# Gate products, the output weight's split and the maxima visits take other places in the prologue of a gated Fourier and attention kernel

## The chip, the cores and the metric

The kernel runs on one core of one Trainium2 chip. Its time is the device time of one execution in microseconds; the time before is the median of three runs.

## The reference

The reference mixes one sequence of 2048 rows of 512 numbers, all in float32, in two ways and blends the results by a gate.

```python
g = _sigmoid((x * gate_w).sum(-1, keepdims=True))
a = dft_seq_re @ (x @ dft_hid_re.T) - dft_seq_im @ (x @ dft_hid_im.T)
q, k, v = heads(x @ wqkv)                  # 32 heads of 16
b = merge(softmax(q @ k.T * 16**-0.5) @ v) @ wo
out = g * a + (1 - g) * b
```

(The lines are shortened; `heads` and `merge` stand for the transposes.)

## The kernel before, in words

Every product in the Fourier part and the projections is made from two parts of each operand, a rounded high part and the rest (`hi_lo`, lines 74 to 76: ScalarE casts the high part, VectorE or GpSimd subtracts for the low part), with three matmuls for each pair (`mm3`, lines 78 to 81). A chain is the twelve matmuls of one 128 x 512 result tile over the four pieces of the inner dimension.

The order of work on every engine is that in which the program issues it; there is no scheduler. The prologue goes in these stages.

1. **q and k**: for each of four blocks of 512 rows (`tb`), four chains of q and four of k. Weights and transposed x come through six `raw` buffers (`staged`, lines 93 to 96) and are split between the chains (`split`, lines 106 to 113; the list of them ends with the imaginary half's weights `wch` and `wcl`). `evac_qk` (lines 136 to 140) splits each result into one of seven `hl` buffers and stores it in DRAM. The gate weights, one row broadcast to 128 partitions (`gwb`), are loaded behind the last chain (line 175).
2. Between the stages SP issues two rows of x for the gate, one of wo, and `load_stacks(0)` (lines 183 to 192): twelve loads that put q and k of the first pair of heads into `qs` and `ks`.
3. **v**: sixteen chains with `wv` (lines 259 to 268); each result is copied to `vt`, one half by ScalarE and one by VectorE.
4. **The imaginary half**: sixteen chains with `wch` (lines 280 to 301). Each result `b` is split into one of two `hl` buffers of a second pool and stored. Behind the b row stands the gate product of row block s on VectorE (line 293, x times `gwb`, summed into column s of `z`) and the load of block s + 2. Behind chains 2 to 5 a piece of wo is split by ScalarE and GpSimd into one of the same two `hl` buffers and stored, and the next is loaded. From the seventh chain on `split(1)` splits a piece of the real half's weights `wre`, which take the memory of `wv`.

`visit(i)` (lines 247 to 257) is called behind chain i of v (0 to 15) and of the imaginary half (16 to 31). From i = 10 on it issues four products of q and k (line 204, 128 x 512 each, three into the banks of `psA` and one into that of `psD`) whose row maxima VectorE takes (line 206); 22 such visits, 44 pairs of tiles, make the lead that the main loop wants. Finished maxima are turned and put beside q by two deferred steps (`m_parts`, `m_rows`), which visits run.

Then the main loop begins with the real half's chains (line 343, into the one bank of `psD`), scores, maxima and values interleaved, and the sequence transform after that. The gate itself is computed once at its beginning (`gate`, lines 611 to 617).

Matmul results go through eight banks: three `s` (`psS`), three `a` (`psA`), one for the values and one `d`. The SP queue issues nearly all transfers, in program order; a transfer that must wait for an engine holds up those behind it.

Of the kernel before, what the change touches and what calls it, by code (L numbers as in the profile page):

```python
# [9 lines left out]
F32 = mybir.dt.float32  # L10
F32R = mybir.dt.float32r
AF = mybir.ActivationFunctionType
ALU = mybir.AluOpType
AX = mybir.AxisListType

P = 128
S = 2048
D = 512
# [3 lines left out]
KT = D // P  # L22
NT = S // P
UNITS = NP * 32
LEAD = 44
# [6 lines left out]
def mix_kernel(ctx: ExitStack, tc: tile.TileContext, xa_t, xa, wqkv, w_hid, w_seq, wo, gate_w, out):  # L32
# [5 lines left out]
    nc = tc.nc  # L38
# [17 lines left out]
    wo_d = [dram.tile([P, 2, D], F32, name=f"wo{kt}") for kt in range(KT)]  # L56
# [5 lines left out]
    z = const.tile([P, NT], F32, name="z")  # L62
# [11 lines left out]
    def hi_lo(hi, lo, src, lo_eng=None):  # L74
        nc.scalar.copy(hi, src)  # L75
        (lo_eng or nc.vector).tensor_tensor(lo, src, hi.bitcast(F32), ALU.subtract)  # L76

    def mm3(ps, sh, sl, mh, ml, first, last):
        nc.tensor.matmul(ps, sh, mh, start=first, stop=False)  # L79
        nc.tensor.matmul(ps, sh, ml, start=False, stop=False)  # L80
        nc.tensor.matmul(ps, sl, mh, start=False, stop=last)  # L81

    right = tc.tile_pool(name="st1", bufs=1, side="right", reuse_waits="tile")
    st1 = right.__enter__()
# [4 lines left out]
    gwb = st1.tile([P, D], F32, name="gwb")  # L89

    todo, loaded = [], []

    def staged(src):
        raw = st1.tile([P, D], F32, name="raw", bufs=RAW)
        nc.sync.dma_start(raw, src)
        return raw

    def add(hi, lo, src, lo_eng, shape=None):
        todo.append((hi, lo, src, lo_eng, shape))

    def load_ahead():
        while todo and len(loaded) < RAW - 1:
            hi, lo, src, lo_eng, shape = todo.pop(0)
            loaded.append((hi, lo, staged(src), lo_eng, shape))

    def split(n):

        for _ in range(n):
            load_ahead()
            if loaded:  # L110
                hi, lo, raw, lo_eng, shape = loaded.pop(0)
                hi_lo(hi, lo, raw.rearrange("p (s t) -> p s t", s=4) if shape else raw, lo_eng)
            load_ahead()

    def add_x(tb, kt):
        x = xab[tb][:, :, :, kt * P:(kt + 1) * P]
        add(x[:, :, 0], x[:, :, 1], xa_t[tb, :, kt], nc.vector, True)
# [3 lines left out]
    def bank():  # L121
        nonlocal banks
        banks += 1
        return (psS if banks % 2 else psA).tile([P, 512], F32, name="s" if banks % 2 else "a")


    with tc.tile_pool(name="qk", bufs=1, reuse_waits="tile") as pool:
        wh = pool.tile([P, 2, KT, D], F32R, name="wh")
        wl = pool.tile([P, 2, KT, D], F32R, name="wl")

        def mm_qk(ps, c, ct, tb, kt):
            cols = slice(ct * P, (ct + 1) * P)
            x = xab[tb][:, :, :, kt * P:(kt + 1) * P]
            mm3(ps, wh[:, c, kt, cols], wl[:, c, kt, cols], x[:, :, 0], x[:, :, 1], kt == 0, kt == KT - 1)

        def evac_qk(ps, c, ct, tb):
            hl = pool.tile([P, 2, D], F32R, name="hl", bufs=7)
            hi_lo(hl[:, 0], hl[:, 1], ps)
            nc.sync.dma_start(qk_d[c][:, ct * P:(ct + 1) * P, tb * 512:(tb + 1) * 512].rearrange("v p t -> p v t"),
                              hl.bitcast(F32))  # L140

        for kt in range(KT):
            add(wh[:, 0, kt], wl[:, 0, kt], wqkv[0, :, kt], nc.vector)
            add_x(0, kt)
        for kt in range(KT):
            add(wh[:, 1, kt], wl[:, 1, kt], wqkv[1, :, kt], nc.vector)
        for tb in range(1, 4):
            for kt in range(KT):
                add_x(tb, kt)
        for kt in range(KT):  # L150
            add(wv[0][kt], wv[1][kt], wqkv[2, :, kt], nc.gpsimd)
        for kt in range(KT):
            add(wch[:, kt], wcl[:, kt], w_hid[1, :, kt], nc.gpsimd)
        split(8)
        nc.vector.memset(acc, 0.0)

        for tb in range(4):
            for c in range(2):
                if tb == 0 and c == 0:
                    pss = [bank() for _ in range(4)]  # L160
                    for kt in range(KT):
                        for ct in range(4):
                            mm_qk(pss[ct], c, ct, tb, kt)
                    split(4)
                    for ct in range(4):
                        evac_qk(pss[ct], c, ct, tb)
                    continue
                for ct in range(4):
                    ps = bank()
                    for kt in range(KT):  # L170
                        mm_qk(ps, c, ct, tb, kt)
                    split(1 if ct % 2 and tb else 2)
                    evac_qk(ps, c, ct, tb)
        split(len(todo) + len(loaded))
        nc.sync.dma_start(gwb, gate_w.broadcast_to([P, D]))

    main = ctx.enter_context(tc.tile_pool(name="main", bufs=1, reuse_waits="tile"))

# [4 lines left out]
    def load_stacks(p):  # L183
        q_t, k_t = qs[p % 2], ks[p % 2]
        for h in range(2):
            rows = slice((2 * p + h) * DH, (2 * p + h + 1) * DH)
            o = 64 * h

            for i, (qv, kv) in enumerate(((0, 0), (0, 1), (1, 0))):
                part = slice(o + 16 * i, o + 16 * i + 16)  # L190
                nc.sync.dma_start(q_t[part].bitcast(F32), qk_d[0][qv, rows])
                nc.sync.dma_start(k_t[part].bitcast(F32), qk_d[1][kv, rows])
# [37 lines left out]
    def run_deferred():  # L230
        while deferred:
            deferred.pop(0)()
# [5 lines left out]
    for i in range(2):  # L238
        for h in range(2):
            for tb in range(2):  # L240
                nc.gpsimd.dma_start(ks[i][64 * h + 48:64 * h + 50, tb * 2 * D:(tb + 1) * 2 * D].bitcast(F32), ones)
    xgs = {s: staged(xa[s]) for s in range(2)}
    wos = [staged(wo[:, 0])]
    load_stacks(0)
    a_next = 0

    def visit(i):

        nonlocal a_next
        if i < 10 or a_next == LEAD:  # L250
            return
        if deferred:
            deferred.pop(0)()
        for j in range(2):
            for h in range(2):
                a_tile(a_next, h, psD.tile([P, 512], F32, name="d") if j and h else None)
            a_next += 1

    for s in range(NT):
        t = xab[s // 4][:, s % 4]  # L260
        ps = psS.tile([P, 512], F32, name="s")
        for kt in range(KT):
            r = slice(kt * P, (kt + 1) * P)
            mm3(ps, t[:, 0, r], t[:, 1, r], wv[0][kt], wv[1][kt], kt == 0, kt == KT - 1)
        visit(s)
        pv = ps.rearrange("p (r h d) -> p r h d", h=2, d=DH)
        nc.scalar.copy(vt[:, s, :, 0:16], pv[:, :, 0])
        nc.vector.tensor_copy(vt[:, s, :, 17:33], pv[:, :, 1])

    def spare(i, dt, name):  # L270

        return const.tile([P, 4, P], dt, name=name, tag=f"w{i}")


    wre = [[const.tile([P, D], F32R, name=f"wre{v}{kt}", tag=f"w{4 * v + kt}") for kt in range(KT)] for v in range(2)]
    for kt in range(KT):
        add(wre[0][kt], wre[1][kt], w_hid[0, :, kt], nc.gpsimd)

    ab = [xab[s // 4][:, s % 4] for s in range(NT)]
    for s in range(NT):  # L280
        t = ab[s]
        ps = psS.tile([P, 512], F32, name="s")
        for kt in range(KT):
            r = slice(kt * P, (kt + 1) * P)
            mm3(ps, t[:, 0, r], t[:, 1, r], wch[:, kt], wcl[:, kt], kt == 0, kt == KT - 1)
        visit(NT + s)
        bt = st1.tile([P, 2, D], F32R, name="hl", bufs=2)
        hi_lo(bt[:, 0], bt[:, 1], ps)
        nc.sync.dma_start(b_d[s], bt.bitcast(F32))
        if s + 2 < NT:  # L290
            xgs[s + 2] = staged(xa[s + 2])
        xg = xgs.pop(s)
        nc.vector.scalar_tensor_tensor(xg, xg, 1.0, gwb, op0=ALU.mult, op1=ALU.mult, accum_out=z[:, s:s + 1])
        if 2 <= s < 2 + KT:
            wt = st1.tile([P, 2, D], F32R, name="hl", bufs=2)
            hi_lo(wt[:, 0], wt[:, 1], wos.pop(0), nc.gpsimd)
            nc.sync.dma_start(wo_d[s - 2], wt.bitcast(F32))
            if s + 1 < 2 + KT:
                wos.append(staged(wo[:, s - 1]))
        elif s >= 2 + KT:  # L300
            split(1)
    run_deferred()
    assert a_next == LEAD
    right.__exit__(None, None, None)
# [108 lines left out]
    oh, yp, wos = {}, {}, []  # L413
# [441 lines left out]
```

## Time and profile before

| | us |
|---|---|
| median of 3 runs | 1752.51 |
| the runs | 1752.32 to 1754.02 |
| the profiled execution | 1753.26 |
| its span, first to last instruction | 1751.5 |

The profile is one execution. Its page gives the busy time of each engine; PE is TensorE's matmuls, PEld its weight loads, DVE VectorE, ACT ScalarE, POOL GpSimd, SP the engine that issues transfers. Its tables of stretches give, for each stretch, every engine's busy time with the count of instructions, the TensorE clock that was granted (PEclk, 1.00 is full), the mean busy share of the 16 DMA engines and the GB/s they moved. A row of the waits reads: engine, line, tile, what it waited for, us in total, times, longest. A row of the timeline reads: start, duration, engine, line, operation, result and operands, shape, count, and in brackets the idle time before it with what ended it. Matmuls are pipelined: the distance between starts, not the duration, is what one costs.

### The profile page before, as it was taken

To read this page: it belongs to the slowest core of one execution; us is meant where nothing else is said; L and a number is where in the kernel's file an instruction comes from. 1 tells how busy PE (TensorE), PEld (TensorE's weight loads), DVE (VectorE), ACT (ScalarE), POOL (GpSimd) and SP (SyncE) were. 2 spreads that over 40 slices of the span, in tenths; PEclk is the share of its full clock that TensorE was granted. 3 is DMA by queue.
4 is the path that set the end of the run, shared out by engine and by line. 5 is a ranking of instruction groups with operands and counts; after the bars stand their busy time and mean duration, and the time that the engine had idled before them with its cause. 6 is when DMAs were issued, how large, how long until landed. Compare 5 with 4: busy or idle time off the path is not lost.

```text
span 1751.5 us, 32890 instructions
## 1 busy us (share of the span) xinstructions
PE 1727.6 (99%) x12721; PEld 1042.1 (59%) x12721; DVE 1368.1 (78%) x2302; ACT 1153.6 (66%) x2257; POOL 447.0 (26%) x561
## 2 busy tenths in 40 slices
PE   8999999999999999999999999999999999999998
PEld 7886554456666666656666666666666566544443
DVE  5228878888888888888888888888888888899953
ACT  5211267776776777776767777767767777777776
POOL 0110222232223233222223243333323333200111
PEclk9999899999999999999999999999999999999999
DMA  8754630304133152414146443314141535461113
GB/s 291 234 113 138 224 42 7 56 21 78 44 62 67 45 123 80 86 55 79 38 80 211 107 127 98 72 57 86 44 85 56 129 98 98 146 168 26 38 27 127
DMA packets 82348, 164.79 MB, mean 94 GB/s; under 512 B 19712, under 2 KB 19968, under 8 KB 78352
## 3 DMA queue, kind: packets, MB, share of 16 engines
q1 hardware_dynamic: 77840, 162.30, 36.4%
q8 instruction: 100, 1.64, 0.4%
q0 software_dynamic: 4352, 0.39, 0.3%
q14 instruction: 56, 0.46, 0.1%
HBM read 107.47 MB, written 54.52 MB: 92 GB/s over the span
## 4 chain that ended last, share of the span: by engine, by line
PE 93%; DVE 2%; ACT 2%; DMA 1%; issue 0%; DVEq 0%; SPq 0%; ACTq 0%
PE d L343 35%; PE acc L638 26%; PE s L629 11%; PE a L204 11%; PE s L79 2%; PE s L80 2%; PE s L81 2%; DVE mx L206 1%; ACT pt L630 1%; DMA b<-hl 1%; PE a L79 1%; PE a L80 1%; PE a L81 1%; ACT y L359 0%; DVE hl L76 0%
## 5 line engine op out<-in xcount | busy, mean ns | idle before, releaser
L206 DVE TENSOR_REDUCE mx<-a 128x1 f32<-128x512 f32 x2026 | 1244.4, 681 | 243.3 <-PE a L204 229.5
L630 ACT ACTIVATE pt<-s 128x512 f32<-128x512 f32 x2008 | 1025.5, 622 | 391.2 <-PE s L629 333.7
L204 PE MATMUL a<-ks,qs 48*128 48x512 f32 x2026 | 814.4, 418 | 3.1 <-DVE mx L206 2.4
L629 PE MATMUL s<-qs,ks 50*128 50x512 f32 x2008 | 769.7, 413 | 0.9 <-ACT pt L630 0.8
L343 PE MATMUL d<-xab,ch 64*128 64x512 f32 x2016 | 648.7, 396 | 0.0
L638 PE MATMUL acc<-pt,vt 128*17 128x512 f32 x4096 | 500.3, 596 | 0.0
L343 PEld LDWEIGHTS d<-xab,ch 64*128 64x128 f32 x2016 | 365.9, 184 | 126.3 <-DVE mx L206 60.4
L629 PEld LDWEIGHTS s<-qs,ks 50*128 50x128 f32 x2008 | 365.6, 184 | 109.1 <-ACT pt L630 30.8
L204 PEld LDWEIGHTS a<-ks,qs 48*128 48x128 f32 x2026 | 366.8, 185 | 77.2 <-DVE mx L206 48.4
L343 PE MATMUL d<-xab,cl 64*128 64x512 f32 x1008 | 399.5, 396 | 0.0
L343 PEld LDWEIGHTS d<-xab,cl 64*128 64x128 f32 x1008 | 185.5, 184 | 64.9 <-DVE mx L206 40.8
L327 POOL CAST ch<-craw 128x512 fp32r<-128x512 f32 x126 | 77.1, 612 | 555.2 <-PE a L204 177.6
L638 PEld LDWEIGHTS acc<-pt,vt 128*17 128x17 f32 x4096 | 90.1, 96 | 206.0 <-issue 206.0
L328 POOL TENSOR_TENSOR cl<-craw,ch 128x512 fp32r<-128x512 f32 x126 | 162.1, 1287 | 10.2
L227 POOL DMA_DIRECT2D qs<-mt x128 | 72.0, 568 | 160.1 <-DVE mt L223 151.6
L343 PE MATMUL d<-wre,xab 64*128 64x512 f32 (+1 forms) x348 | 95.1, 406 | 5.0 <-ACT pt L630 2.5
L343 PEld LDWEIGHTS d<-wre,xab 64*128 64x128 f32 (+1 forms) x348 | 59.9, 185 | 42.6 <-issue 26.1
L343 PE MATMUL d<-wo_hl,o_hl 64*128 64x512 f32 (+1 forms) x261 | 71.0, 398 | 0.0
L343 PEld LDWEIGHTS d<-wo_hl,o_hl 64*128 64x128 f32 (+1 forms) x261 | 47.1, 185 | 15.9 <-issue 11.7
L75 ACT CAST hl<-s 128x512 fp32r<-128x512 f32 x32 | 18.7, 585 | 56.8 <-PE s L81 49.5
L76 DVE TENSOR_TENSOR hl<-s,hl 128x512 fp32r<-128x512 f32 x32 | 22.0, 687 | 35.0 <-ACT hl L75 35.0
L218 POOL CAST nhl<-nm 128x16 fp32r<-128x16 f32 x32 | 6.3, 197 | 151.2 <-DVE nm L215 151.2
(125 smaller groups left out, 931.8 us busy)
## 6 DMA issues: line engine op xcount, KB each, us to landing
craw<-w_seq SPq DMA_DIRECT2D x128, 256.0 KB
qk<-hl SPq DMA_DIRECT2D x32, 512.0 KB
qs<-qk SPq DMA_DIRECT2D x96, 128.0 KB
ks<-qk SPq DMA_DIRECT2D x96, 128.0 KB
b<-hl SPq DMA_DIRECT2D x16, 512.0 KB
xab<-b SPq DMA_DIRECT2D x16, 512.0 KB
o<-oe SPq DMA_DIRECT2D x62, 128.0 KB
oh<-nh SPq DMA_DIRECT2D x12, 512.0 KB
```

What stands on the lines that cost most here:

```text
L79: nc.tensor.matmul(ps, sh, mh, start=first, stop=False)
L80: nc.tensor.matmul(ps, sh, ml, start=False, stop=False)
L81: nc.tensor.matmul(ps, sl, mh, start=False, stop=last)
L204: nc.tensor.matmul(ps, qs[p % 2][r, qt * P:(qt + 1) * P], ks[p % 2][r, kb * 512:(kb + 1) * 512], start=True, stop=True)
L206: user = nc.vector.tensor_reduce(mx[p % 2][:, h, qt, kb:kb + 1], ps, AX.X, ALU.max)
L227: (nc.sync, nc.gpsimd)[h].dma_start(rows.rearrange("v (q b c) -> v b q c", q=8, b=4)[:, b], mt[hf][32 * b + h:32 * b + 32:2])
L327: nc.gpsimd.tensor_copy(h1, raw)
L328: nc.gpsimd.tensor_tensor(l1, raw, h1.bitcast(F32), ALU.subtract)
L343: i = nc.tensor.matmul(self.ps, st[r], mv[r], start=not self.begun, stop=stop)
L629: nc.tensor.matmul(ps, ks[p % 2][rr, kt * P:(kt + 1) * P], qs[p % 2][rr, q0:q0 + 512], start=True, stop=True)
L630: return nc.scalar.activation(pts[u][:, 2 * qb + h], ps, AF.Exp, bias=0.0, scale=DH ** -0.5)
L638: nc.tensor.matmul(acc[32 * j:32 * j + 17], vt[:, kt, p, 16 * h:16 * h + 17], pt[:, j], start=kt == 0, stop=kt == NT - 1)
```

## The change

- The gate products move from behind the chains of the imaginary half to behind the last sixteen chains of q and k. The gate weights and five rows of x are loaded ahead of those chains, and each product is followed by the load of the row block five further on.
- The splits of wo move from behind chains 2 to 5 of the imaginary half to behind chains 6, 8, 10 and 12 of v; their four loads are issued together behind `load_stacks(0)`. Behind each store of a wo piece a piece of the real half's weights is loaded, and these are split behind the first four chains of the imaginary half.
- The visits issue maxima from i = 7 on instead of i = 10; their number stays 22, so the last is behind chain 28 and not 31. A visit runs a deferred step even when it has no maxima to issue.

```diff
+        xgs = {}
+        def gate_row(s):
+            xg = xgs.pop(s)
+            nc.vector.scalar_tensor_tensor(xg, xg, 1.0, gwb, op0=ALU.mult, op1=ALU.mult, accum_out=z[:, s:s + 1])
+            if s + 5 < NT:
+                xgs[s + 5] = staged(xa[s + 5])
+
         for tb in range(4):
+            if tb == 2:
+                assert not todo and not loaded
+                nc.sync.dma_start(gwb, gate_w.broadcast_to([P, D]))
+                xgs.update({s: staged(xa[s]) for s in range(5)})
...
                     evac_qk(ps, c, ct, tb)
-        split(len(todo) + len(loaded))
-        nc.sync.dma_start(gwb, gate_w.broadcast_to([P, D]))
+                    if tb > 1:
+                        gate_row(8 * (tb - 2) + 4 * c + ct)
...
-    xgs = {s: staged(xa[s]) for s in range(2)}
-    wos = [staged(wo[:, 0])]
     load_stacks(0)
+    wos = [staged(wo[:, kt]) for kt in range(KT)]
+    wrs = []
...
     def visit(i):
-        if i < 10 or a_next == LEAD:
-            return
         if deferred:
             deferred.pop(0)()
+        if i < 7 or a_next == LEAD:
+            return
...
         nc.vector.tensor_copy(vt[:, s, :, 17:33], pv[:, :, 1])
+        if s in range(6, 14, 2):
+            kt = (s - 6) // 2
+            wt = st1.tile([P, 2, D], F32R, name="hl", bufs=2)
+            hi_lo(wt[:, 0], wt[:, 1], wos.pop(0), nc.gpsimd)
+            nc.sync.dma_start(wo_d[kt], wt.bitcast(F32))
+            wrs.append(staged(w_hid[0, :, kt]))
...
-    for kt in range(KT):
-        add(wre[0][kt], wre[1][kt], w_hid[0, :, kt], nc.gpsimd)
...
         hi_lo(bt[:, 0], bt[:, 1], ps)
         nc.sync.dma_start(b_d[s], bt.bitcast(F32))
-        if s + 2 < NT:
-            xgs[s + 2] = staged(xa[s + 2])
-        xg = xgs.pop(s)
-        nc.vector.scalar_tensor_tensor(xg, xg, 1.0, gwb, op0=ALU.mult, op1=ALU.mult, accum_out=z[:, s:s + 1])
-        if 2 <= s < 2 + KT:
-            wt = st1.tile([P, 2, D], F32R, name="hl", bufs=2)
-            hi_lo(wt[:, 0], wt[:, 1], wos.pop(0), nc.gpsimd)
-            nc.sync.dma_start(wo_d[s - 2], wt.bitcast(F32))
-            if s + 1 < 2 + KT:
-                wos.append(staged(wo[:, s - 1]))
-        elif s >= 2 + KT:
-            split(1)
+        if s < KT:
+            hi_lo(wre[0][s], wre[1][s], wrs.pop(0), nc.gpsimd)
```

## The prediction

> **What bounds the kernel now.** I read the totals first, then the waits by stage (the table of stretches over the prologue), then the chain that ended last, then single instructions of the stretch that stood out.
>
> ```profile
> span 1751.5 us, 32890 instructions
> PE 1727.6 (99%) x12721; PEld 1042.1 (59%) x12721; DVE 1368.1 (78%) x2302; ACT 1153.6 (66%) x2257; POOL 447.0 (26%) x561
> ...
> PE 93%; DVE 2%; ACT 2%; DMA 1%; issue 0%; DVEq 0%; SPq 0%; ACTq 0%
> ```
>
> TensorE carries 93% of the chain. What is to be had lies in the other 7%, and in stretches where TensorE counts as busy at a lower clock. The change touches the prologue alone, and the stretches show where that loses time.
>
> ```profile
> core 0: us, PE busy (x) PEld busy (x) DVE busy (x) ACT busy (x) POOL busy (x), PEclk, DMA share, GB/s
> 51.00:98.00 47.00, 47.00 (x209) 38.89 (x209) 11.76 (x17) 10.64 (x19) 2.77 (x3) 1.00 0.67 202
> 107.00:111.00 4.00, 4.00 (x19) 3.30 (x19) 0.42 (x1) 0.38 (x1) 0.00 (x0) 1.00 1.06 129
> 125.00:144.00 19.00, 19.00 (x86) 12.90 (x86) 14.45 (x26) 2.29 (x6) 0.00 (x0) 1.00 0.00 1
> 144.00:168.00 24.00, 24.00 (x106) 16.50 (x106) 21.48 (x42) 4.17 (x7) 3.02 (x2) 1.00 0.53 183
> 168.00:196.00 28.00, 25.24 (x72) 15.50 (x70) 17.95 (x37) 6.69 (x12) 8.41 (x8) 0.82 0.70 246
> 196.00:217.00 21.00, 18.57 (x83) 12.50 (x82) 21.00 (x41) 3.07 (x6) 2.33 (x4) 1.00 0.60 203
> 240.00:1700.00 1460.00, 1455.13 (x11481) 854.28 (x11479) 1217.78 (x2036) 1048.63 (x2060) 403.27 (x511) 1.00 0.33 78
> ```
>
> Up to 168 us TensorE is full. From 168 to 196, in the chains of the imaginary half (wch), it issues 72 matmuls in 28 us where the 24 us before held 106, at a mean granted clock of 0.82. From 196 to 217 VectorE is busy for all 21 us. From 240 to 1700 TensorE is full again, so what is won before should not be absorbed there. The chain says what stalls the middle:
>
> ```profile
> 157.71 2.92 DMA b<-hl
> 162.06 3.33 DMA b<-hl
> 166.97 5.08 DMA b<-hl
> 173.81 5.09 DMA b<-hl
> 181.26 4.20 DMA raw<-w_hid
> ```
>
> and the table of waits, from 95 to 217 us:
>
> ```profile
> ACT hl L75 <- DMA raw<-wo: 12.4, 3, 4.9
> ACT hl L75 <- DMA b<-hl: 9.5, 6, 3.1
> ACT wre L75 <- DMA raw<-w_hid: 6.1, 2, 5.9
> PE d L343 <- DVE mx L206: 2.4, 1, 2.4
> ```
>
> ScalarE's casts of b rows queue behind casts of wo rows that wait for their load (line 296), and wo parts and b rows share the two hl buffers (lines 287 and 295). VectorE then gets the b rows late, the next maxima behind them, and TensorE waits for the banks.
>
> **Part by part.** The pitch of the chains comes from the timeline of TensorE.
>
> ```profile
> 95.04 0.39 PE L79 MATMUL s<-wv,xab 128*128 128x512 f32 x1
> 97.76 0.39 PE L79 MATMUL s<-wv,xab 128*128 128x512 f32 x1
> ...
> 125.05 0.73 PE L204 MATMUL a<-ks,qs 48*128 48x512 f32 x3
> 128.65 0.73 PE L204 MATMUL a<-ks,qs 48*128 48x512 f32 x3
> ...
> 144.56 0.40 PE L79 MATMUL s<-wch,xab 128*128 128x512 f32 x1
> 145.26 0.40 PE L79 MATMUL s<-wch,xab 128*128 128x512 f32 x1
> ...
> 146.75 0.73 PE L204 MATMUL a<-ks,qs 48*128 48x512 f32 x3
> 150.41 0.73 PE L204 MATMUL a<-ks,qs 48*128 48x512 f32 x3
> ...
> 213.72 0.73 PE L204 MATMUL a<-ks,qs 48*128 48x512 f32 x3
> ...
> 216.89 1.64 PE L343 MATMUL d<-wre,xab 128*128 128x512 f32 x6 [2.43 <-DVE mx L206]
> ```
>
> A plain chain of v takes 97.76 - 95.04 = 2.72 us, one with a visit 128.65 - 125.05 = 3.60, so a visit costs 0.88. In wch three matmuls take 0.70, a plain chain 4 x 0.70 = 2.80; with a visit 150.41 - 146.75 = 3.66.
>
> *Visits from the eighth chain.* The first visit (a maxima block of four products) moves from behind the eleventh chain of v, at 125.05, to behind the eighth, at 125.05 - 3 x 2.72 = 116.89. Three more visits lie in v, and the last three wch chains have none. TensorE does the same products, 3 x 0.88 there against 3 x 0.86 here: nothing by itself. But the main loop's first d product need no longer wait the 2.43 us for the last visit's maxima.
>
> *Gate products.* Sixteen VectorE products leave wch for the last sixteen chains of q and k.
>
> ```profile
> L293 DVE SCALAR_TENSOR_TENSOR raw<-raw,gwb 128x512 f32<-128x512 f32 x15 | 10.3, 686 | 0.0
> L76 DVE TENSOR_TENSOR hl<-s,hl 128x512 fp32r<-128x512 f32 x16 | 10.9, 682 | 11.1 <-ACT hl L75 11.1
> L206 DVE TENSOR_REDUCE mx<-a 128x1 f32<-128x512 f32 x66 | 41.4, 682 | 7.7 <-PE a L204 7.7
> L76 POOL TENSOR_TENSOR hl<-raw,hl 128x512 fp32r<-128x512 f32 x4 | 5.6, 1398 | 67.7 <-DMA raw<-xa 51.4 <-ACT hl L75 16.3
> ```
>
> A VectorE step of this size is 682 to 686 ns. With the gate product a wch chain has six of them, up to 4.1 us against a pitch of 3.66 (consecutive ones overlap a little, which is why 3.66 could just hold); without it five, 3.4 us, and TensorE sets the pace. In q and k VectorE has 11.76 us of work in 47; adding 16 x 0.69 = 11 us leaves it at about half. The new wait is that of the first product for the gate row and the first x row, issued just before it: a load like it took 4.20 us above. Behind it on VectorE queues the next chain's low part, and behind that its store. Seven hl buffers, one per chain of 2.72 us, and five further banks cover that: only a lateness beyond some 5 x 2.72 = 13 us would reach TensorE. I cost it at nothing.
>
> *Loads moved.* The 16 row loads and the gate row (17 x 0.262 = 4.46 MB) now share the queue of SP and the engines with the q and k stores. From 51 to 98 us the engines are 0.67 busy: (1 - 0.67) x 47 = 15.5 us free. The load rate is not shown for these in that stage. The nearest row is that of the opening, nearly all loads of this form:
>
> ```profile
> 4.00:18.00 14.00, 12.65 (x45) 9.98 (x46) 8.93 (x14) 8.32 (x14) 0.00 (x0) 1.00 0.82 279
> ```
>
> 279 / 0.82 = 340 GB/s at full use, so 4.46 / 0.34 = 13.1 us: it fits, barely. The far bound is the stack loads at 107 to 111, 129 / 1.06 = 122 GB/s: 36.6 us, which does not fit. I take the near one, as these are 128-row loads like the opening's; the far one stays as a rival. The Trainium skill, "DMA: Bandwidth & Descriptors", section "Bandwidth", speaks against the edit: small transfers are inefficient, measured there at 138 GB/s for 64 KB and 341 for 1 MB. At its lower figure these loads would be an estimated 32 us and overflow the stage; the opening's 256 KB loads, several in flight, run at the rate of its 1 MB row.
>
> What a late queue would hurt is the stack loads (qs, ks), which the first visit needs:
>
> ```profile
> 96.98 0.46 SPq L175 DMA_DIRECT2D gwb<-gate_w  x1
> ...
> 101.44 0.31 SPq L192 DMA_DIRECT2D ks<-qk  x1
> ...
> 109.57 0.30 SPq L192 DMA_DIRECT2D ks<-qk  x1
> ...
> 115.00:117.00 2.00, 2.00 (x10) 1.68 (x9) 0.12 (x1) 0.01 (x1) 0.00 (x0) 1.00 0.16 29
> ```
>
> They land by about 116 now, behind four transfers issued from 96.98 on (gate row, two x rows, one wo: 1.05 MB, 3 us at 340 GB/s). Those are gone from that place: the stacks should land at 113 to 114, 3 us ahead of the visit at 116.89.
>
> *wo split and real-half loads.* Four ScalarE casts, four GpSimd parts (1.4 us each), four stores and eight loads move to v, where ScalarE is busy 2.29 us of 19 and GpSimd 0. The wo loads are issued behind the stacks; the first cast comes behind chain seven, at about 114, and can wait a little, with the vt copies queued behind it: the three s banks let TensorE run on for two chains, 5.4 us. The real half's rows are then loaded well before their casts in the first four wch chains. So the three ScalarE waits of 12.4, 9.5 and 6.1 us go, with the hl buffers used by b rows alone: a store of 2.9 to 3.3 us per pitch of 3.66, two buffers. Next in line is TensorE.
>
> *Sum.* The first visit of wch moves from 146.75 to 146.75 + 3 x 0.88 = 149.39. Twelve pitches of 3.66 to the last visit: 193.31. That visit with its following chain, 3.66, and two plain chains, 5.60: 202.57. The first d product is at 216.89 now: 14.3 us less. Checked from the other side: from 146.75 to 213.72 there are fifteen pitches, 54.9 us, taking 66.97: 12.1 lost; then 216.89 - 213.72 - 0.93 for four products = 2.2. Together 14.3. Of it, 28 x (1 - 0.82) = 5.0 us is the lowered clock. The profiled execution took 1753.26 us (span and 1.76), so 1738.9; the median is 0.75 lower, so **1738.2**.
>
> **The clock.** The longest wait of TensorE in the thinned stretch is short:
>
> ```profile
> 174.73 1.69 PE L204 MATMUL a<-ks,qs 48*128 48x512 f32 x3 [1.39 <-DVE mx L206]
> ```
>
> and still the mean clock of 168 to 196 is 0.82. The Trainium skill, "TensorE: Matmul & The Clock Gate", "Part 1: The HAM clock gate", has the fall come after an idle window of about 3.4 us; by that rule these gaps would not cause the fall, and filling them would not bring the lost clock back. The trace speaks against the rule: no gap is that long, and the clock is 1.00 on either side of the thinned stretch, so I take thin issue as the cause and the 5.0 us as won; were it another, the sum would be 1743.2, rival (b).
>
> **Rivals.**
> (a) *Part of the gain* (0.17): the eighth chain finds the stacks 1 to 4 us late, or the end of wch waits for b stores, two buffers at a pitch of 2.80. For: only 3 us of margin. Against: lighter traffic before. 1739 to 1743.
> (b) *The clock stays low* for another cause (0.04): 1738.2 + 5.0 = 1743.2. For it the row of 0.82 alone.
> (c) *Slower* (0.04): row loads at the stack loads' 122 GB/s. 36.6 us against 15.5 free: 21 us of backlog at 98, less the 1.05 MB that leaves (8.6 at that price): stacks land at 116 + 12.5 = 128.5, and TensorE stands 11.6 us at the first visit, then pays up to the 5.0 us that the lower clock cost above: 16.6 lost against 14.3 won, 1754.8. It decides where the loads run below 133 GB/s (3.41 MB net then exceed the 15.5 us by 10.2, which puts the stacks at 126.2 and the loss at 14.3).
> (d) *No change* (0.02): the main loop is held by something not moved, the stream of w_seq loads. Against: TensorE busy 1455 of 1460 us. 1752.5.
>
> **How the numbers follow.** The full gain has 0.73 and gives 1738.2; its own range is 1736.5 (wch at v's pitch, 16 x 0.06 less, and 0.75 for the spread between executions) to 1739.5. The range reaches to (a) and (b): 1736.5 to 1743.2, leaving out (c), (d) and some of the first. A measurement can tell 0.2%, 3.5 us. Faster 0.73 + 0.17 + 0.04 = 0.94; same 0.02; slower 0.04.
>
> **What would show it.** Right: the first maxima block at 117 us without a wait for ks or qs; no wait of ScalarE for wo, w_hid or b of more than 1 us; clock 1.00 throughout 143 to 203; first d product at 202 to 203; from there on the same distances as before. Wrong: TensorE idle at 117, VectorE late in q and k with hl waits there, b stores on the chain, or a main loop longer than before by what was won.

## The result, and the profile after

The changed kernel takes 1738.96 us (median of four runs, 1738.34 to 1740.25) against 1752.57 for the kernel before (also four runs): a ratio of 0.9912, 95% interval 0.9899 to 0.9925. The profiled execution took 1738.59 us with a span of 1736.8, against 1753.26 and 1751.5. The prediction was 1738.2 in a range of 1736.5 to 1743.2.

The page of the profile after, totals and chain:

```profile
span 1736.8 us, 32902 instructions
PE 1717.9 (99%) x12721; PEld 1036.8 (60%) x12721; DVE 1368.8 (79%) x2302; ACT 1153.1 (66%) x2257; POOL 447.3 (26%) x561
...
PE 96%; ACT 2%; DVE 1%; DMA 0%; issue 0%; POOL 0%; DVEq 0%; SPq 0%; ACTq 0%; POOLq 0%
```

TensorE's share of the chain went from 93% to 96%; its count of matmuls is the same. The stretches of the prologue, same columns as before:

```profile
51.00:98.00 47.00, 47.00 (x210) 38.89 (x208) 21.67 (x50) 10.45 (x19) 2.77 (x3) 1.00 0.91 300
144.00:168.00 24.00, 24.00 (x107) 16.06 (x106) 19.49 (x33) 5.98 (x11) 5.16 (x4) 1.00 0.23 90
168.00:196.00 28.00, 28.00 (x124) 19.22 (x124) 24.22 (x42) 4.11 (x7) 2.76 (x6) 1.00 0.38 149
```

From 168 to 196 TensorE issues 124 matmuls where it issued 72, with the clock at 1.00 instead of 0.82. VectorE has 24.22 us of work in these 28, so it is no longer behind. The price stands in the first row: the transfer engines are 0.91 busy in the q and k stage instead of 0.67, with TensorE still full. The places of the visits and of the first d product, on TensorE's timeline after:

```profile
116.22 0.73 PE L217 MATMUL a<-ks,qs 48*128 48x512 f32 x3
119.84 0.73 PE L217 MATMUL a<-ks,qs 48*128 48x512 f32 x3
...
201.82 1.53 PE L349 MATMUL d<-wre,xab 128*128 128x512 f32 x6
```

No wait is in brackets: neither for the stacks at the first visit nor for VectorE at the first d product. That product starts 216.89 - 201.82 = 15.1 us earlier, the span ends 14.7 us earlier: the main loop keeps nearly all that the prologue won. Of the ScalarE waits for transfers from 95 to 217 us these are left. They are longer than the 1 us that the prediction named as its sign, but TensorE is busy without a break through the stages in which they fall:

```profile
ACT hl L75 <- DMA b<-hl: 4.6, 2, 2.7
ACT hl L75 <- DMA raw<-wo: 2.2, 1, 2.2
```

### The profile page after: what moved, and what is told of

Same layout as the page of the kernel before. It is cut to its first block, busy times and chain, and to the rows that moved or that the text cites. A ratio compares the mean times of both kernels' runs of the same rounds, so it can differ in the third digit from the quotient of the medians.

```text
span 1736.8 us, 32902 instructions
## 1 busy us (share of the span) xinstructions
PE 1717.9 (99%) x12721; PEld 1036.8 (60%) x12721; DVE 1368.8 (79%) x2302; ACT 1153.1 (66%) x2257; POOL 447.3 (26%) x561
## 3 DMA queue, kind: packets, MB, share of 16 engines
q8 instruction: 100, 1.64, 0.4%
## 4 chain that ended last, share of the span: by engine, by line
PE 96%; ACT 2%; DVE 1%; DMA 0%; issue 0%; POOL 0%; DVEq 0%; SPq 0%; ACTq 0%; POOLq 0%
PE d L349 35%; PE acc L644 26%; PE s L635 12%; PE a L217 12%; PE s L79 3%; PE s L80 3%; PE s L81 3%; ACT pt L636 1%; PE a L79 1%; PE a L81 1%; PE a L80 1%; ACT y L365 0%; DVE mx L219 0%; PE a L349 0%; DMA qs<-mt 0%
## 5 line engine op out<-in xcount | busy, mean ns | idle before, releaser
L349 PEld LDWEIGHTS d<-wo_hl,o_hl 64*128 64x128 f32 (+1 forms) x261 | 47.1, 185 | 16.2 <-issue 11.7
L366 POOL CAST xab<-y 128x512 fp32r<-128x512 f32 x16 | 9.8, 613 | 136.9 <-ACT y L365 108.9
```

What stands on the lines that cost most here:

```text
L349: i = nc.tensor.matmul(self.ps, st[r], mv[r], start=not self.begun, stop=stop)
```

## The experiments

The theory tested (A) was the prediction's: the loss comes from the wo splits among the b rows. Its rival (B): VectorE's six steps a chain are the bound there. The change has three parts: gate products (G), wo splits and real-half loads (W), visits (V). Six kernels have one or two of them, so that the table holds every combination. Median times are from different chips, on which the kernel before had medians of 1752.6 to 1755.4 with a wide spread, while the changed kernel gave 1738.96 and 1739.25 on two of them. So a difference of 1 or 2 us between kernels is read from the profiles, and not from the medians alone.

| parts | ratio (95%) | median us | span us | first d product at us |
|---|---|---|---|---|
| none | 1 | 1752.57 | 1751.5 | 216.89 |
| G | 0.9976 (0.9966 to 0.9985) | 1751.93 | 1750.7 | 214.09 |
| V | 1.0002 (0.9992 to 1.0012) | 1754.66 | 1751.5 | 216.86 |
| G, V | 0.9978 (0.9966 to 0.9991) | 1751.14 | 1749.5 | 215.41 |
| W | 0.9929 (0.9913 to 0.9946) | 1743.42 | 1741.5 | 204.59 |
| G, W | 0.9928 (0.9913 to 0.9943) | 1743.20 | 1741.3 | 204.87 |
| W, V | 0.9932 (0.9917 to 0.9946) | 1741.02 | 1739.8 | 202.66 |
| G, W, V | 0.9912 (0.9899 to 0.9925) | 1738.96 | 1736.8 | 201.82 |

**Gate products alone.** `gate_row` and its loads as in the change, all else as before.

> The kernel before with the gate products alone moved behind the last chains of q and k. Theory A (the waits come from the wo splits among the b rows: late wo loads and two shared hl buffers; VectorE's six steps a chain only just hold the pitch): those waits stay, thinned by the x rows that no longer share the transfer engines; the wait before the first d product stays. 3 to 6 us below the kernel before, 1747 to 1750. Theory B (VectorE's six steps a chain are the bound of these chains): most of the gain, 10 us or more, 1740 to 1743.

Measured 1751.93, ratio 0.9976. The median lies above A's values, the ratio would put it at 1748.4 and within them; B is out either way. The waits of ScalarE stayed:

```profile
ACT hl L75 <- DMA raw<-wo: 11.0, 3, 5.0
ACT hl L75 <- DMA b<-hl: 9.5, 5, 3.0
ACT wre L75 <- DMA raw<-w_hid: 6.0, 1, 6.0
```

The first d product comes 2.8 us earlier, but the span is only 0.8 us shorter: behind the wait before that product the clock fell, to 0.70 from 213 to 217 us.

**wo splits and real-half loads alone.**

```diff
 # in the chains of v
+        if s in range(6, 14, 2):
+            ...  hi_lo(wt[:, 0], wt[:, 1], wos.pop(0), nc.gpsimd); store; wrs.append(staged(w_hid[0, :, kt]))
+        if s == 13:
+            xgs.update({i: staged(xa[i]) for i in range(2)})
 # in the imaginary half's chains
+        if s < KT:
+            hi_lo(wre[0][s], wre[1][s], wrs.pop(0), nc.gpsimd)
+        gate_row(s)
```

> The kernel before with the wo splits and the real half's loads alone moved, gate products behind the imaginary half's chains, visits from the eleventh chain. Theory A: the pitch is 3.66 to 3.7 us throughout, clock 1.00, only the wait of 2.2 us before the first d product stays: 1740.5 to 1742. Theory B: VectorE at six steps makes the pitch 4.0 or so for 16 chains, 5 to 6 us more: 1746 to 1748.

Measured 1743.42, 1 to 2 us above A's span of values and well below B's. The stretches and the end of its stage:

```profile
168.00:196.00 28.00, 28.00 (x124) 18.81 (x123) 28.00 (x57) 4.69 (x8) 2.75 (x6) 1.00 0.63 214
...
205.00:209.00 4.00, 4.00 (x13) 2.53 (x13) 1.95 (x9) 1.07 (x3) 0.00 (x0) 0.64 0.91 224
...
204.59 1.62 PE L347 MATMUL d<-wre,xab 128*128 128x512 f32 x3 [2.43 <-DVE mx L214]
```

VectorE, with its six steps, is busy for all 28 us and yet TensorE issues its full 124 matmuls: both just hold the pitch of 3.66. The steps last 0.68 us each but start 0.60 apart in this trace, so six of them fit. The remainder over A is in the last two rows. The 2.43 us wait at the end stayed, and here the clock fell behind it, to 0.64 from 205 to 209.

**Visits alone**, `if i < 7` in place of `if i < 10`.

> The kernel before with the visits alone moved, from the eighth chain on. Theory A: the middle waits stay; the last three chains have no maxima, so the first d product does not wait: 2 to 3 us below the kernel before, 1749.5 to 1750.5. Theory B: three chains fewer that VectorE holds up, the same 2 to 4 us. A third (the stacks are late for the eighth chain, behind four other loads): they land at about 116 for a visit at 116.9, and if late TensorE stands there 1 us, so 1751.

Measured 1.0002: nothing, a miss for all three. The first d product no longer waits for maxima, but starts at 216.86, where it started before. The stalls in the middle took up what the end gave: the visit behind chain 28 starts at 207.70 here and at 202.75 in the kernel before. The first visit also met the stacks late:

```profile
118.07 0.51 PE L212 MATMUL a<-ks,qs 48*128 48x512 f32 x2 [0.55 <-DMA ks<-qk]
```

**Gate products and wo splits, visits as before** (`if i < 10` in the changed kernel).

> The changed kernel with visits from the eleventh chain on, as before. Theory A: the 2.2 us before the first d product come back and nothing else: 1740.5 to 1741.5. Theory B: the same or less, as VectorE has one step fewer and is not behind: 1739 to 1741.

Measured 1743.20, some 2 us above both: the end wait and the clock again.

```profile
204.87 2.67 PE L349 MATMUL d<-wre,xab 128*128 128x512 f32 x6 [2.43 <-DVE mx L219]
```

Six products take 2.67 us here against 1.53 in the changed kernel. G beside W without V is worth 0.2 us of span, which is nothing that a run can tell.

**Gate products and visits, wo splits as before.**

> The changed kernel with the wo splits and the real half's splits put back among the imaginary half's chains. Theory A: the waits of ScalarE for wo, b and w_hid come back, and with them thin issue and the lower clock, less the share of the x rows; the end is free: 1744 to 1748. Theory B (VectorE's six steps were the bound): almost nothing comes back, 1738.5 to 1740.

Measured 0.9978, 1751.14: B is out, and more came back than A said (3 us above its values). Beside G alone, V added nothing that the ratios can tell here either.

**wo splits and visits, gate products as before.**

> The changed kernel with the gate products put back behind the imaginary half's chains. Theory A: the pitch stays at 3.66 to 3.7, so 1739 to 1740.5 (the last products stand behind the last three chains, where VectorE has time). Theory B: pitch of 4.0 or so for 13 chains, 4 to 5 us: 1743 to 1744.

Measured 1741.02, 0.5 above A's values and 2 below B's. Its first d product stands 0.84 us behind that of the changed kernel, but the six steps of VectorE are not the reason. The loss is there at the second visit:

```profile
116.59 0.99 PE L212 MATMUL a<-ks,qs 48*128 48x512 f32 x3
120.68 0.73 PE L212 MATMUL a<-ks,qs 48*128 48x512 f32 x3
```

The first visit starts 0.37 us later than in the changed kernel, less than the 0.48 us by which two profiles of the changed kernel differ there, and the second follows it by 4.09 us instead of 3.62. From the second visit to the first d product both kernels take 82.0 us. So the gate products cost nothing beside the b rows here. Of the other 2 us of span, about 1 stands between the first and the third d product (5.43 us apart instead of 4.45), where ScalarE waits 1.36 us for the last gate product before it can compute the gate. The rest is about what the clock lost in this one profile from 1672 to 1676 us, where it was 0.62; it is 1.00 at that place in the changed kernel, and what lowered it was not settled.

**The first visit two chains earlier still** (`if i < 5`).

> The changed kernel with the first visit behind the sixth chain of v instead of the eighth, at 110.8 us by its trace. If the stacks land at 113 to 114, TensorE stands 2.5 to 3 us there and nothing is won at the end: 1741.5 to 1742, and some more if the clock falls. If the margin was larger than thought (landing before 111): no change, 1738.5 to 1739.5.

Measured 1747.61, ratio 0.9965: TensorE did wait, but for 4.81 us instead of the 2.5 to 3 expected, and paid again in clock. SP's issue of the first k load, the wait, and the stretches around it:

```profile
100.55 0.31 SPq L205 DMA_DIRECT2D ks<-qk  x1
...
116.62 0.79 PE L217 MATMUL a<-ks,qs 48*128 48x512 f32 x2 [4.81 <-DMA ks<-qk]
...
117.00:121.00 4.00, 4.00 (x11) 2.68 (x10) 2.22 (x4) 0.00 (x0) 0.00 (x0) 0.50 0.06 22
121.00:125.00 4.00, 4.00 (x16) 2.65 (x15) 1.49 (x3) 0.89 (x2) 0.94 (x1) 0.79 0.00 0
```

The visit gets its stacks 116.62 - 100.55 = 16.1 us behind the issue of the first k load, not 12 or so. The first d product was at 210.47, 8.65 us late for a wait of 4.81.

**Row loads twice.** Behind each gate product in q and k

```diff
+                        nc.sync.dma_start(spareb[j % 4], xa[j])
```

> The changed kernel with every gate row of x loaded a second time, behind its product, into a spare buffer that nobody reads: 4.2 MB more in the q and k stage. The first 4.46 MB raised the busy share from 0.67 to 0.91 there; so much again overflows by 0.15 x 47 = 7 us, the stacks land at about 120 instead of 113 to 114, and TensorE stands 3 to 4 us at the first visit: 1742 to 1743. If the seven hl buffers and the queue take it up: 1739. If transfers run at the stack loads' rate once the engines are full (the prediction's slower rival): 30 us more, 1755 or above.

Measured 1741.16 (1739.11 to 1746.93), ratio 0.9943: too wide to place, but the profile is plain.

```profile
51.00:98.00 47.00, 47.00 (x209) 38.92 (x208) 21.40 (x49) 10.66 (x19) 2.78 (x4) 1.00 1.02 374
```

The engines are at 1.02 and move 374 GB/s, and TensorE is still full; the first visit waits 0.56 us for the stacks and not 3 to 4, and the first d product comes at 203.46, 1.64 late. So the stage took up most of the 4.2 MB more: (374 - 300) x 47 = 3.5 MB.

**What the wo splits cost where they stood.** Three splits of part W on the kernel before, run beside the changed kernel, which gave 1739.25 and 0.9911 (0.9895 to 0.9926) again.

> The changed kernel as it is, beside the three splits of its wo part. 1738 to 1740, a ratio of 0.991 to 0.993; it ties the comparisons of the other chips to this one.

Own buffers for the wo parts:

```diff
-            wt = st1.tile([P, 2, D], F32R, name="hl", bufs=2)
+            wt = st1.tile([P, 2, D], F32R, name="wt", bufs=2)
```

> The kernel before, its wo parts in two buffers of their own instead of the b rows' two hl buffers; loads and places unchanged. Shared buffers: while bt and wt take turns, each b row waits for the store of the one before (cast to landing 4 to 6 us against a pitch of 3.66), so 4 to 6 us should go: 1747 to 1749. Late loads: the wait of ScalarE for the wo loads (12.4 us in three waits) stays and holds the b casts as before: 1751 to 1753. Crowded transfers (neither, the engines are simply full): 1752 to 1755.

Measured 0.9989 (0.998 to 0.9998), 1753.77. The shared buffers alone are out. The time does not tell late loads from crowded transfers, but the trace speaks for late loads: the waits for b stores went down from 9.5 us to 2.2, while those for wo loads (10.7) and the real half's rows (8.1) stayed, with the transfer engines 0.73 busy from 168 to 196 us and so not full. All four wo loads early, in four buffers of their own:

```diff
-    wos = [staged(wo[:, 0])]
     load_stacks(0)
+    wos = [st1.tile([P, D], F32, name=f"wraw{kt}") for kt in range(KT)]
+    for kt in range(KT):
+        nc.sync.dma_start(wos[kt], wo[:, kt])
```

> The kernel before, its four wo loads issued together behind the stacks into four buffers of their own; splits and stores unchanged. Late loads as the cause: the waits for wo go, and most of the loss with them, 1743 to 1746. Shared buffers: b rows still wait for the store before, 4 to 6 us of loss stay, 1747 to 1749. Crowded transfers: 1752 to 1755.

Measured 0.9977 (0.9967 to 0.9987), 1750.96, in none of the three ranges (the ratio would put it at 1748.5, in that of shared buffers) and well above that of late loads alone: the waits for wo went, and waits for stores (8.0 and 6.4 us) and for the real half's rows (6.8) stood in their place. Both edits together:

> Both of the last two edits on the kernel before: early wo loads and own buffers, splits still among the b rows. If these two waits are the whole of what moving the splits brought, it stands with the run that moved them alone, 1742.5 to 1744.5 on its scale (ratio 0.993). If the place beside the b rows costs by itself (casts, GpSimd parts, stores in the same chains): 1746 or more.

Measured 0.9968 (0.9955 to 0.998), 1749.70, a little under half of what W alone brings; the expectation that these two are the whole failed. Its trace shows what is left, first on TensorE, then on ScalarE, then TensorE again:

```profile
171.80 0.73 PE L204 MATMUL a<-ks,qs 48*128 48x512 f32 x3
175.46 0.73 PE L204 MATMUL a<-ks,qs 48*128 48x512 f32 x3
...
178.93 0.62 ACT L75 CAST wre<-raw 128x512 fp32r<-128x512 f32 x1 [9.74 <-DMA raw<-w_hid]
...
182.11 1.95 PE L204 MATMUL a<-ks,qs 48*128 48x512 f32 x3 [2.92 <-DVE mx L206]
190.04 0.79 PE L204 MATMUL a<-ks,qs 48*128 48x512 f32 x3
```

Visits keep the pitch of 3.66 through 175.46, right through the wo splits. Then the first cast of the real half's rows waits 9.74 us for a load issued only when `split` comes to it; the next b casts queue behind it on ScalarE, and two visits slip to 6.65 and 7.93 us. So there were three waits in a row, each hiding the next: wo loads, shared buffers, real-half loads. Part W takes all three away; a kernel with early real-half loads on top of these two edits was not tried.

## Why the prediction was right, point by point

*The bound and the sum.* The reading that these waits of ScalarE starve VectorE, and VectorE TensorE, held: W by itself brings 10.0 of the 14.7 us of span. The sum from pitches, 14.3, stands against 15.1 at the first d product and 14.7 over the span; 0.67 of the 0.8 more at the first d product is there at the first visit already, 116.22 instead of 116.89. It worked because it did not add up stalls, which hide each other, but counted what TensorE would do with none.

*Gate products.* Costed as a step that only just fitted, not the cause, and that held: from the second visit to the first d product they cost nothing beside W, with V or without it. What their move brings beside W and V lies elsewhere, in the 1 us at the start of the main loop above. The first one waited in q and k as foreseen, without reaching TensorE:

```profile
DVE raw L162 <- DMA raw<-xa: 3.5, 1, 3.5
```

*Price of the row loads.* Mis-sized on the safe side: forecast 13.1 us of full engines at 340 GB/s. Busy share times time went from 0.67 x 47 to 0.91 x 47, 11.3 us more for (300 - 202) x 47 = 4.6 MB, that is 408 GB/s. The 138 GB/s that the Trainium skill, "DMA: Bandwidth & Descriptors", section "Bandwidth", measured for 64 KB did not apply to these loads of 256 KB with several in flight.

*Stacks ahead of the first visit.* This step failed, and that its result held was luck. "They land by about 116 now" read the last faint transfers of one row; the gap of 3 us it promised is not there. With 16.1 us from the first k load (the run with the visit two chains earlier), and that load here at

```profile
99.99 0.31 SPq L205 DMA_DIRECT2D ks<-qk  x1
```

the stacks land at an estimated 116.1, for a visit at 116.22. Where the first visit comes 16.2 us or more behind the first k load (this kernel, and G with V), it loses nothing; at 15.9 us (W with V) it loses 0.47, and at 15.3 and 15.2 (V alone, the row loads twice) 1.0. Rival (a) deserved more than 0.17.

*Visits.* Sized at the 2.2 us wait at the end. Beside G and W they brought 4.5 us of span: 2.43 for the wait, some 1.7 for the clock that fell behind it (0.57 over 4 us), which the sum did not have, and a rest no larger than two profiles of one kernel differ by. Without W they brought nothing clear, as the stalls ahead absorbed it.

*The clock.* Rival (b) is out: with the waits gone the clock is 1.00 from 144 to 203. Whether thin issue as such lowered it before, as the prediction has it, or its single gaps did, no run separates. Rival (c) would have needed loads at under 133 GB/s, and they ran at 408; rival (d), a main loop that gives the gain back, is out by the 14.7 us of span.

## What to carry to other kernels

When an in-order engine serves both a critical stream and a side job, the side job's late load is a wait in the critical stream; move the whole job, loads first, to a stage where that engine and the transfers are idle. Where several waits follow each other, taking away one shows almost nothing; predict from the pitch that is left with none, and test by the whole group. And read when a load has landed from who waited for it, not from the tail of a traffic row.

## What the runs showed of the hardware that was not expected

The clock falls after short waits, but not after each. The same wait of 2.43 us stands before the first d product in seven of the kernels; behind it the clock fell in four and stayed at 1.00 in three. It was 0.64 with W alone (above), and 0.57 and 1.00 in these two, with G and W and in the kernel before:

```profile
205.00:209.00 4.00, 4.00 (x12) 2.30 (x13) 1.18 (x6) 0.69 (x2) 0.00 (x0) 0.57 0.65 194
...
217.00:221.00 4.00, 4.00 (x18) 2.53 (x20) 2.92 (x9) 1.47 (x4) 0.00 (x0) 1.00 0.66 201
```

The Trainium skill, "TensorE: Matmul & The Clock Gate", "Part 1: The HAM clock gate", has the clock fall after an idle window of about 3.4 us, and that window run freely. The fall behind the 4.81 us wait agrees; those behind 2.43 us are shorter than its rule allows. That the same wait does and does not cost the clock says that more than its length counts, such as where a free-running window stands when it begins; no run here sets that, so it is not shown.
